# A kernel of attention and two feed-forward layers: the first pass's order is taken from a table of pieces, and ScalarE takes over squares, scaling and sums

## The chip, the cores and the metric

The kernel runs on one core of a Trainium2 chip. The metric is the device time of one execution in microseconds (us). The engines that matter are TensorE (PE in the profile; PEld is its loading of weights), VectorE (DVE), ScalarE (ACT), GpSimd (POOL) and SyncE (SP), which issues transfers. Each engine works through its own list of instructions in the order in which the program holds them; an instruction that waits holds up all that stand behind it on that engine.

## What is computed

```python
scores = scale * q_c @ k_c^T              # q, k, v: (4, 8, 576, 64), chunks of 64 positions
attn   = exp(scores - rowmax);  attn /= (rowsum + 1e-9)
x      = attn @ v_c                       # put together as 2304 tokens x 512
x      = (s * relu(x @ w_in)**2 + b) @ w_out       # layer 1, 512 -> 2048 -> 512
h      = x @ w2_in
out    = (h * tanh(softplus(h))) @ w2_out          # layer 2 (Mish)
```

All in float32; the matrix products of the layers are made of three products each, of a high and a low part (hi*hi, hi*lo, lo*hi).

## The kernel before

The 2304 tokens are 18 attention tiles of 128, and five blocks of 512, 256, 512, 512 and 512 tokens for the layers. The 2048 inner columns of a layer are 16 chunks of 128; four chunks form a group, and one pass takes one group through all five blocks. So there are eight passes (four for each layer) of 20 steps. A step is one chunk on one block: 12 matmuls into a hidden tile `hp` (`mm_in`, L331), the squaring or Mish, the splitting into `ghi` and `glo`, and 12 matmuls into the accumulators (`mm_out`, L368). At the end of a block the accumulators are added into `ysum` (L383 to L387).

In the first pass the attention runs beside layer 1. Each tile goes through: K and Q transposed on TensorE (`k_pe`, `q_pe`, L231) and copied out by ScalarE (L243 into the block diagonal `kbd`, L252 into `qt`); the scores (`s_pe`, L263); maximum and subtraction on VectorE (L274, L275); the exponential on ScalarE (L281); sum, reciprocal and normalising (L286 to L290, the last on GpSimd for three early tiles and on VectorE for the others); the result transposed (L231) and copied (L298); the product with V (`x_pe`, L308); and the hi and lo parts of x (L314 on ScalarE, L315 on VectorE). The weights are decoded from their loaded words as well: `abs` on ScalarE (L124), two clamps and shifts and two combinations on VectorE (L129 to L144), hi on ScalarE (L157), lo on VectorE (L162).

The order before comes from two hand-written strings and a loop. `LOADS` (L22) lists the first transfers, with V of tiles 0 to 3 issued from ScalarE's queue. `START` (L23) orders the first four tiles, with some dummy matmuls on zeros (`w3` is three of them) between the pieces. Then the loop at L468 takes one layer step after another; in step n it also does X of tile n+1, T (the transpose of the weights of the attention) of tile n+2, S of tile n+3, and K and Q of tile n+4. The rest of the first pass (three steps) and all the later passes are written at L528, and the framework's scheduler orders them. The PSUM banks of the loop's attention are two (`ps_t`), handed out in turn.

Of the kernel before, what the change touches and what calls it, by code (L numbers as in the profile page):

```python
# [15 lines left out]
P = 128  # L16
# [5 lines left out]
LOADS = "k0 q0 V0 k1 q1 V1 k2 q2 V2 W0 k3 q3 V3 W1 k4 q4 W2 W3 s0 k5 q5 v4 W4 W5 v5 W6 W7 v6"  # L22
START = (  # L23
    "w3 w5 K0 k0* Q0 q0 w3 K1 S0 k1* Q1 w1 m0 q1 e0 S1 n0 Q2 K2 K3 k2 m1 q2 e1 T0 S2 w3 n1 m2 Q3 k3 q3 T1 "
    "e2 t0 n2 t1 S3 X0 m3 T2 e3 X1 n3* A0 x0 w4 t2 T3 x1 t3 X2 A1 x2 B0 X3 w2 x3 w6 B1"
# [7 lines left out]
def chunk_attention_moe_moe_kernel(  # L33
# [44 lines left out]
    ps_t = ctx.enter_context(tc.tile_pool(name="ps_t", bufs=2, space=bass.MemoryType.PSUM))  # L78
# [7 lines left out]
    def x_tiles(b):  # L86
        xhi[b] = sb.tile([P, KD, sizes[b]], F32R, tag=f"xhi{b}", name=f"xhi{b}")
        xlo[b] = sb.tile([P, KD, sizes[b]], F32R, tag=f"xlo{b}", name=f"xlo{b}")

    def y_tile(b):  # L90
        ysum[b] = sb.tile([P, KD * sizes[b]], F32, tag=f"ysum{b}", name=f"ysum{b}")
# [18 lines left out]
    def decode_w(l, f, part):  # L110
        decode_a(l, f, part)
        decode_b(l, f, part)

    def decode_a(l, f, part):
        decode_a1(l, f, part)
        decode_a2(l, f, part)

    def decode_a1(l, f, part):
# [3 lines left out]
        u = a.bitcast(U32)  # L122
        if l == 1:
            nc.scalar.activation(out=a, in_=t[:, :, 1].bitcast(F32), func=AF.Abs)  # L124
        else:
            nc.vector.tensor_scalar(
                out=u, in0=t[:, :, 1], scalar1=0x7FFFFFFF, scalar2=None, op0=ALU.bitwise_and
            )
        nc.vector.tensor_scalar(  # L129
# [7 lines left out]
    def decode_a2(l, f, part):  # L137
# [36 lines left out]
    kbd = {}  # L174
# [53 lines left out]
    def transposes(i, src):  # L228
        p = ps_at(i, [P, KD, P])
# [16 lines left out]
    def q_pe(i):
        at[i]["qp"] = transposes(i, at[i]["q"].rearrange("p h d -> p (h d)"))

    def q_out(i, alt=False):
        at[i]["qt"] = sb_at(i, "qt").rearrange("p (a s) -> p a s", a=KD)  # L250
        eng = nc.vector.tensor_copy if alt else nc.scalar.copy
        eng(out=at[i]["qt"], in_=at[i].pop("qp"))  # L252
        if NS <= i and i + 2 < NTILE:
            load_qk(i + 2, "k")
            load_qk(i + 2, "q")

    def s_pe(i):
        t = at[i]
        t["sp"] = ps_at(i, [P, H, CH])
# [50 lines left out]
    def x_out(i, alt=False):  # L310
        xp = at.pop(i)["xp"]
        b, o = home[i]
        hi, lo = xhi[b][:, :, o:o + P], xlo[b][:, :, o:o + P]
        nc.scalar.activation(out=hi, in_=xp, func=AF.Copy)  # L314
        nc.vector.tensor_tensor(out=lo, in0=xp, in1=hi.bitcast(F32), op=ALU.subtract)  # L315
        if NS <= i and i + 3 < NTILE:
            load_v(i + 3)


    def mm_in(l, f, b, spare):  # L320

        n = sizes[b]
        pool, tag = (ps_t, "t") if spare and f % 2 else (ps_h, "h")
# [14 lines left out]
    def ew_a(l, hp, n):  # L338
        r = sb.tile([P, TB], F32, tag="tmp", bufs=2, name="r")[:, :n]
        if l == 1:  # L340
            nc.scalar.activation(out=r, in_=hp, func=AF.Relu)  # L341
            nc.vector.scalar_tensor_tensor(  # L342
                out=r, in0=r, scalar=s_sb[:, 0:1], in1=r, op0=ALU.mult, op1=ALU.mult
            )
# [4 lines left out]
    def ew_b(l, r, n):  # L349
        hi = sb.tile([P, TB], F32R, tag="ghi", bufs=3, name="ghi")[:, :n]  # L350
        lo = sb.tile([P, TB], F32R, tag="glo", bufs=3, name="glo")[:, :n]
        if l == 1:
            nc.scalar.activation(out=r, in_=r, func=AF.Identity, bias=b_sb[:, 0:1])  # L353
        nc.scalar.activation(out=hi, in_=r, func=AF.Copy)  # L354
        nc.vector.tensor_tensor(out=lo, in0=r, in1=hi.bitcast(F32), op=ALU.subtract)  # L355
        return hi, lo
# [17 lines left out]

    def add_up(l, grp, b, acc):

        t0, n = blocks[b]
        for m, a in enumerate(acc):
            w = n if l == 1 else DM
            y = ysum[b][:, m * w:(m + 1) * w]  # L380
            if grp == 0:
                if m % 2:
                    nc.vector.tensor_copy(out=y, in_=a[:, :w])  # L383
                else:
                    nc.scalar.copy(out=y, in_=a[:, :w])
# [18 lines left out]

    pend = []
    accs = {}

    def out_half(h):
        l, grp, b, f, g = pend[0]
        if h == 0 and f % FG == 0:  # L410
            accs[l, b] = [
                ps_acc.tile([P, TB], F32, tag=f"acc{m}", name=f"acc{m}")
                for m in range(KD if l == 1 else sizes[b] // P)
            ]
        mm_out(l, f, g, accs[l, b], sizes[b], h)
        if h == 1:
            pend.pop(0)
            if f % FG == FG - 1:
                add_up(l, grp % NG, b, accs.pop((l, b)))

    first, second = chunk_parts(0), chunk_parts(1)
    DECODE = {0: first[2:4], 1: first[4:6], 2: first[6:7], 3: first[7:8]}
    DECODE.update(zip((7, 9, 10, 11, 13, 14, 15, 16), ([z] for z in second)))
    with tc.manual_schedule():
        nc.scalar.preload_act_table_set("exp_and_others")
# [153 lines left out]
```

## Time and profile before

| | us |
|---|---|
| median of 3 runs | 922.19 (921.17 to 923.06) |
| the profiled execution | 922.06 |
| its span, first to last instruction | 920.3 |
| TensorE busy in the span | 880.0 (96%) |
| VectorE busy | 480.9 (52%) |
| ScalarE busy | 368.7 (40%) |
| last matmul ends at | 915.86 |

The span is read by stages: TensorE has idle time only before 203 us; from there to 915.86 us it is busy without a gap, and 4.4 us of last additions and stores follow. The 1.8 us between the span and the time of the execution lie around the program.

### The profile page before, as it was taken

The page shows a single profiled execution, that of the slowest core. Times are in us where ns is not written, and L with a number is a line of the kernel's source. Part 1 is how long each engine was busy: PE and PEld are TensorE (multiplying, and loading weights), DVE is VectorE, ACT ScalarE, POOL GpSimd, SP SyncE. Part 2 cuts the span into 40 slices and gives each one's busy share as a digit, 9 for nine tenths or more (in the row PEclk, how much of TensorE's full clock was granted, in tenths as well). Part 3 has the DMA queues.
Part 4 walks back from the last instruction along what each step waited for, and adds up shares of the span by engine and source line. Part 5 has one row for each costly group of instructions (what it writes and reads, how often), then busy time and mean ns, then how long its engine had stood idle before and what let it go on. Part 6 is the DMA issues. An engine that isn't in the chain of part 4 may idle for free.

```text
span 920.3 us, 12036 instructions
## 1 busy us (share of the span) xinstructions
PE 880.0 (96%) x4878; PEld 735.8 (80%) x4878; DVE 480.9 (52%) x851; ACT 368.7 (40%) x643; POOL 33.9 (4%) x33
## 2 busy tenths in 40 slices
PE   4878889999999999999999999999999999999998
PEld 4656777778888888888988888888888888888886
DVE  1767667768833694359635971166225932222223
ACT  1555556656543463334544542233222322222221
POOL 1100000000000000000212220000000000000000
PEclk7978999999999999999999999999999999999999
DMA  9524463205000410023001400041003200001012
GB/s 251 149 47 115 121 162 98 46 1 160 24 1 1 124 59 1 1 69 115 1 1 37 125 22 1 5 133 46 0 1 93 90 1 1 0 1 46 24 46 91
DMA packets 81526, 53.20 MB, mean 58 GB/s; under 512 B 58688, under 2 KB 75072, under 8 KB 81472
## 3 DMA queue, kind: packets, MB, share of 16 engines
q1 hardware_dynamic: 77120, 51.39, 19.1%
q10 hardware_dynamic: 4352, 1.05, 0.5%
q8 instruction: 38, 0.62, 0.3%
q14 instruction: 16, 0.13, 0.0%
HBM read 47.71 MB, written 4.72 MB: 57 GB/s over the span
## 4 chain that ended last, share of the span: by engine, by line
PE 82%; DVE 9%; ACT 5%; DMA 2%; issue 1%; POOL 0%; DVEq 0%; ACTq 0%; POOLq 0%
PE hp L331 41%; PE acc L368 39%; DMA v<-in_v_dram 2%; DVE wdec L144 1%; DVE wdec L140 1%; ACT e L281 1%; ACT kbd L243 1%; ACT w L157 1%; DVE sm L286 1%; DVE e L275 1%; DVE xlo L315 1%; DVE mx L274 1%; DVE e L290 1%; DVE w L162 1%; DVE wdec L132 1%
## 5 line engine op out<-in xcount | busy, mean ns | idle before, releaser
L331 PE MATMUL hp<-xhi,w 128*128 128x512 f32 (+1 forms) x1280 | 373.1, 373 | 2.6 <-ACT w L157 1.7
L331 PEld LDWEIGHTS hp<-xhi,w 128*128 128x128 f32 x1280 | 233.3, 190 | 47.1 <-issue 2.7
L331 PE MATMUL hp<-xlo,w 128*128 128x512 f32 (+1 forms) x640 | 237.6, 371 | 0.1
L355 DVE TENSOR_TENSOR glo<-r,ghi 128x512 fp32r<-128x512 f32 (+1 forms) x160 | 104.9, 656 | 215.3 <-ACT ghi L354 214.9
L368 PE MATMUL acc<-ghi,w 128*128 128x512 f32 (+1 forms) x640 | 164.8, 375 | 2.5 <-DVE w L162 1.9
L368 PE MATMUL acc<-w,ghi 128*128 128x512 f32 x576 | 159.6, 390 | 0.0
L346 ACT ACTIVATE r<-hp 128x512 f32<-128x512 f32 (+1 forms) x80 | 44.4, 555 | 255.1 <-PE hp L331 255.1
L331 PEld LDWEIGHTS hp<-xlo,w 128*128 128x128 f32 x640 | 121.6, 190 | 21.6 <-DVE xlo L315 0.8
L368 PEld LDWEIGHTS acc<-ghi,w 128*128 128x128 f32 x640 | 113.7, 190 | 22.1 <-DVE w L162 2.2
L368 PEld LDWEIGHTS acc<-w,ghi 128*128 128x128 f32 x576 | 106.9, 188 | 21.3
L387 DVE TENSOR_TENSOR ysum<-acc,ysum 128x512 f32<-128x512 f32 (+1 forms) x114 | 71.8, 655 | 59.5 <-PE acc L368 59.5
L341 ACT ACTIVATE r<-hp 128x512 f32<-128x512 f32 (+1 forms) x80 | 44.1, 551 | 132.1 <-PE hp L331 132.0
L354 ACT ACTIVATE ghi<-r 128x512 fp32r<-128x512 f32 (+1 forms) x160 | 94.1, 588 | 4.5
L368 PE MATMUL acc<-glo,w 128*128 128x512 f32 (+1 forms) x320 | 94.1, 370 | 0.0
L368 PE MATMUL acc<-w,glo 128*128 128x512 f32 x288 | 93.9, 389 | 0.0
L342 DVE SCALAR_TENSOR_TENSOR r<-r,s_sb 128x512 f32<-128x512 f32 (+1 forms) x80 | 56.4, 705 | 67.3 <-ACT r L341 67.2
L353 ACT ACTIVATE r<-r,b_sb 128x512 f32<-128x512 f32 (+1 forms) x80 | 54.6, 682 | 51.2 <-DVE r L342 51.0
L368 PEld LDWEIGHTS acc<-glo,w 128*128 128x128 f32 x320 | 58.4, 189 | 10.3
L368 PEld LDWEIGHTS acc<-w,glo 128*128 128x128 f32 x288 | 54.1, 188 | 11.3
L157 ACT ACTIVATE w<-wdec 128x512 fp32r<-128x512 f32 x64 | 40.3, 630 | 54.4 <-DVE wdec L144 54.0
L162 DVE TENSOR_TENSOR w<-wdec,w 128x512 fp32r<-128x512 f32 x64 | 44.9, 703 | 2.9 <-ACT w L157 2.0
L140 DVE SCALAR_TENSOR_TENSOR wdec<-wraw,wdec 128x512 uint32<-128x512 uint32 x64 | 44.0, 693 | 0.6
(302 smaller groups left out, 494.7 us busy)
## 6 DMA issues: line engine op xcount, KB each, us to landing
wraw<-in_moe_w_in_dram SPq DMA_DIRECT2D x32, 512.0 KB, 3.9
wraw<-in_moe_w_out_dram SPq DMA_DIRECT2D x32, 512.0 KB, 3.5
out_dram<-ysum SPq DMA_DIRECT2D x18, 256.0 KB, 2.0
k<-in_k_dram SPq DMA_DIRECT2D x16, 256.0 KB, 2.9
v<-in_v_dram SPq DMA_DIRECT2D x56, 64.0 KB, 3.3
q<-in_q_dram SPq DMA_DIRECT2D x12, 256.0 KB, 2.9
v<-in_v_dram ACTq DMA_DIRECT2D x16, 64.0 KB, 4.1
k<-in_q_dram SPq DMA_DIRECT2D x4, 256.0 KB, 4.8
```

The lines of the kernel that those rows point to most:

```text
L140: nc.vector.scalar_tensor_tensor(out=u, in0=t[:, :, 1], scalar=0xC0000000, in1=u, op0=ALU.bitwise_and, op1=ALU.bitwise_or,)
L157: nc.scalar.activation(out=w[:, 0], in_=a, func=AF.Copy)
L162: nc.vector.tensor_tensor(out=lo, in0=a, in1=hi.bitcast(F32), op=ALU.subtract)
L331: nc.tensor.matmul(out=hp, lhsT=w[:, sl], rhs=r[b][:, a, :], start=(a == 0 and p == 0), stop=(a == KD - 1 and p == 2),)
L341: nc.scalar.activation(out=r, in_=hp, func=AF.Relu)
L342: nc.vector.scalar_tensor_tensor(out=r, in0=r, scalar=s_sb[:, 0:1], in1=r, op0=ALU.mult, op1=ALU.mult)
L346: nc.scalar.activation(out=r, in_=hp, func=AF.Mish)
L353: nc.scalar.activation(out=r, in_=r, func=AF.Identity, bias=b_sb[:, 0:1])
L354: nc.scalar.activation(out=hi, in_=r, func=AF.Copy)
L355: nc.vector.tensor_tensor(out=lo, in0=r, in1=hi.bitcast(F32), op=ALU.subtract)
L368: nc.tensor.matmul(out=acc[m][:, :n] if l == 1 else acc[m], lhsT=w[wi][:, sl] if l == 1 else g[gi][:, sl], rhs=g[gi] if l == 1 else w[wi], ...
L387: nc.vector.tensor_tensor(out=y, in0=a[:, :w], in1=y, op=ALU.add)
```

## The change

The strings `LOADS` and the loop are gone. A new `START` names every piece of the whole first pass in one order, transfers included, and a function `pieces` issues them. A name is a kind and a number: `dk`, `dq`, `dv` are the loads of a tile; `K Q S T X` its parts on TensorE with `@` the PSUM bank; `k q m e n z t x y` the parts on ScalarE and VectorE (`z` is the normalising, now on VectorE for all tiles); `W a c d h l` load and decode a weight part; `I J` and `O P` are the halves of `mm_in` and `mm_out` of a step, `r u v g o` its elementwise parts, `E` the copy of an accumulator into `ysum`; `w13` is thirteen dummy matmuls. In all there are 76 dummy matmuls in the table, where there were 27.

Further: the squares of steps 0 to 7 are an `activation` with Square on ScalarE (`u`), and their scaling by s goes into the activation that adds b (`v`); the accumulators of blocks 0 and 1 are copied by ScalarE alone; three `kbd` buffers serve all tiles in turn, where tiles from 4 on had one; the attention uses up to six PSUM banks that the table names; V of tiles 1 to 3 is loaded from SyncE's queue; the first pass ends wholly before the second pass begins, and the last three of the 16 weight parts that the first pass decoded are decoded at the beginning of the second (`rest`).

```diff
-LOADS = "k0 q0 V0 k1 q1 V1 k2 q2 V2 W0 k3 q3 V3 W1 k4 q4 W2 W3 s0 k5 q5 v4 W4 W5 v5 W6 W7 v6"
 START = (
-    "w3 w5 K0 k0* Q0 q0 w3 K1 S0 k1* Q1 w1 m0 q1 e0 S1 n0 Q2 K2 K3 k2 m1 q2 e1 T0 S2 w3 n1 m2 Q3 k3 q3 T1 "
+    "dq0 dk0 dv0 W2 dk2 dq2 dq1 Q0@4 dk1 q0 w3 K0@5 dk3 k0.0 dq3 sb dv2 w13 S0@0 a2 c2 w2 K2@1 m0 k2.1 dq8 w3 "
...
+    "n7 J5 r3 O0 z9 r5 u3 z7 Q16@5 u5 m10 v3 P0 dq15 v5 q16 c7 I4 e10 K12@4 c4 g3 I7 k12.0 dk15 o3 J4 n10 J7 r4 "
...
-        eng = nc.gpsimd if i < NS and not alt else nc.vector
-        eng.tensor_tensor(out=e, in0=e, in1=sm.to_broadcast([P, H, CH]), op=ALU.mult)
...
+    def s_norm(i):
+        e = at[i]["e"]
+        nc.vector.tensor_tensor(out=e, in0=e, in1=at[i].pop("sm").to_broadcast([P, H, CH]), op=ALU.mult)
...
+    def ew_v(r, squared=False):
+        nc.scalar.activation(
+            out=r, in_=r, func=AF.Identity, scale=s_sb[:, 0:1] if squared else 1.0, bias=b_sb[:, 0:1]
+        )
...
+        elif name == "dv":
+            load_v(i, nc.sync if i else nc.scalar)
...
+        elif name == "u":
+            if i < 8:
+                nc.scalar.activation(out=ff[i]["r"], in_=ff[i]["r"], func=AF.Square)
+            else:
+                ew_u(ff[i]["r"])
...
+        elif name == "E":
+            first_sum(i, m, first_acc[i][m], nc.vector.tensor_copy if m % 2 and i >= 2 else nc.scalar.copy)
...
-    for grp in range(2 * NG):
+    for grp in range(1, 2 * NG):
...
+        rest = parts[13:] if grp == 1 else []
...
+            for z in rest[2 * step:2 * step + 2]:
+                decode_w(*z)
```

Where instructions stand now is shown at three places. First TensorE at the very start; `warm` is the output of the dummy matmuls, `ident` the identity of the transposes. Before:

```order
L445 MATMUL warm<-zero 128x128 x8
L231 MATMUL pa<-ident,k 128x128 x8
L445 MATMUL warm<-zero 128x128 x3
L231 MATMUL pa<-ident,k 128x128 x4
L263 MATMUL pa<-kbd,v 64x128 x8
```

and now:

```order
L246 MATMUL pt__103<-ident,q 128x128 x4
L468 MATMUL warm<-zero 128x128 x3
L246 MATMUL pt__113<-ident,q 128x128 x4
L468 MATMUL warm<-zero 128x128 x13
L272 MATMUL pa<-kbd,v 64x128 x8
L468 MATMUL warm<-zero 128x128 x2
```

The eight dummy matmuls that stood ahead of the first transposes are gone, and thirteen stand between the transposes of tile 0 and its scores.

Second, ScalarE at the start; L243 and now L257 are the copies that the first scores need. Before:

```order
L425 ACT_TABLE_LOAD
L224 DMA v<-in_v_dram 64x4x64 x16
L243 COPY kbd<-pa 64x8x64
L252 COPY v<-pa 128x512
L243 COPY kbd_161<-pa 64x8x64
```

and now:

```order
L498 ACT_TABLE_LOAD
L238 DMA v<-in_v_dram 64x4x64 x4
L264 COPY v<-pt__103 128x512
L257 COPY kbd<-pt__113 64x8x64 x2
L140 ACTIVATE wdec<-wraw 128x512
```

Twelve of the sixteen transfers that stood ahead of the first copy have left ScalarE's list (they are on SyncE's now).

Third, TensorE in the middle of the first pass: how a tile's small matmuls (L231, L263, L308) lie among those of the layer. Before, from block 1:

```order
L231 MATMUL pt__891<-ident,q 128x128 x4
L308 MATMUL pt__904<-e,v 64x64 x16
L331 MATMUL hp<-xhi_438,w 128x256 x2
L331 MATMUL hp<-xlo_439,w 128x256
...
L263 MATMUL pt__935<-kbd,qt 64x128 x8
L331 MATMUL hp<-xhi_438,w 128x256 x2
```

and now, ahead of the first use of the accumulators:

```order
L246 MATMUL pt__922<-ident,e 128x128 x4
L246 MATMUL pa<-ident,q 128x128 x4
L318 MATMUL pt__941<-e,v 64x64 x16
L246 MATMUL pa<-ident,k 128x128 x4
L272 MATMUL pt__979<-kbd_83,qt 64x128 x8
L318 MATMUL pa<-e,v 64x64 x16
L246 MATMUL pa<-ident,k 128x128 x4
L272 MATMUL pa<-kbd,qt 64x128 x8
L344 MATMUL hp<-xhi_321,w 128x512 x2
```

The small matmuls of several tiles now stand in a row, and there are fewer places at which TensorE goes over from them to the layer's.

## Rows read from the trace of the kernel before

**Rows 1.** Busy time by stretch: start:end, length, then each engine's busy us (instructions), clock, DMA.

```profile
0.00:202.89 202.89, 167.08 (x1513) 136.87 (x1513) 127.63 (x238) 105.74 (x192) 7.39 (x13) 0.92 0.44 112
106.00:202.89 96.89, 88.12 (x854) 71.46 (x852) 67.42 (x127) 58.21 (x108) 0.00 (x0) 1.00 0.35 88
202.89:915.86 712.97, 712.97 (x3366) 598.96 (x3366) 352.16 (x613) 262.97 (x452) 26.55 (x20) 1.00 0.13 41
135.06:144.44 9.38, 9.38 (x89) 7.51 (x85) 7.13 (x13) 5.08 (x10) 0.00 (x0) 1.00 0.35 95
207.40:212.84 5.44, 5.44 (x26) 4.50 (x25) 3.95 (x7) 3.07 (x6) 0.00 (x0) 1.00 0.56 151
242.75:244.19 1.44, 1.44 (x14) 1.43 (x12) 1.40 (x4) 0.74 (x2) 0.00 (x0) 1.00 0.00 0
157.17:166.87 9.70, 9.44 (x85) 7.49 (x85) 7.65 (x16) 5.72 (x10) 0.00 (x0) 1.00 0.40 90
217.78:244.09 26.31, 26.31 (x123) 21.98 (x123) 26.07 (x49) 18.88 (x33) 0.00 (x0) 1.00 0.28 89
```

**Rows 2.** Waits of TensorE, first 202 us: us in total, times, longest us.

```profile
PE pa L263 <- DVE kbd L243: 10.8, 1, 10.8
PE pt__519 L263 <- ACT qt L252: 3.7, 1, 3.7
```

**Rows 3.** Timeline of ScalarE's queue at the start: start us, us, instruction, count.

```profile
0.76 16.24 ACTq L224 DMA_DIRECT2D v<-in_v_dram  x16
```

**Rows 4.** Timeline of TensorE around step 16 of the first pass.

```profile
202.89 0.73 PE L331 MATMUL hp<-xhi,w 128*128 128x512 f32 x2 [0.94 <-ACT xhi L314]
```

**Rows 5.** Timeline of TensorE: small matmuls of a tile, each with the row behind it.

```profile
136.65 1.09 PE L263 MATMUL pt__1366<-kbd,qt 128*64 128x128 f32 x16
137.68 0.73 PE L331 MATMUL hp<-xhi,w 128*128 128x512 f32 x2
...
141.00 0.60 PE L231 MATMUL pt__1415<-ident,k 128*128 128x128 f32 x4
141.35 0.71 PE L368 MATMUL acc<-ghi,w 128*128 128x512 f32 x2
...
143.36 1.15 PE L308 MATMUL pt__1445<-e,v 64*64 64x64 f32 x32
144.44 0.73 PE L331 MATMUL hp<-xhi,w 128*128 128x512 f32 x2
```

**Rows 6.** Timeline of TensorE: dummy matmuls (two records each) and the first transposes.

```profile
1.05 3.79 PE L445 MATMUL warm<-zero 128*128 128x128 f32 x16 [1.05 <-DVE zero L439]
4.63 1.92 PE L231 MATMUL pa<-ident,k 128*128 128x128 f32 x8
...
38.37 2.05 PE L445 MATMUL warm<-zero 128*128 128x128 f32 x16
```

**Rows 7.** Timeline of VectorE within one step.

```profile
157.96 0.68 DVE L274 TENSOR_REDUCE mx<-pt__1590 128x8 f32<-128x512 f32 x1
...
159.29 0.74 DVE L342 SCALAR_TENSOR_TENSOR r<-r,s_sb 128x512 f32<-128x512 f32 x1
160.07 0.69 DVE L286 TENSOR_REDUCE sm<-e 128x8 f32<-128x512 f32 x1
...
161.23 0.69 DVE L290 TENSOR_TENSOR e<-e,sm 128x512 f32<-128x512 f32 x1
161.84 0.69 DVE L355 TENSOR_TENSOR glo<-r,ghi 128x512 fp32r<-128x512 f32 x1
```

**Rows 8.** ScalarE's activation of line 354, first 260 us: ns min/median/max.

```profile
L354 ACT ACTIVATE ghi<-r x28: 417/632/635, 49.3 to 257.1; 128x512 fp32r<-128x512 f32 x20, 128x256 fp32r<-128x256 f32 x8
```

**Rows 9.** Transfers of the first 35 us, and SyncE's issue of one tile's V.

```profile
DMA packets 22242, 8.96 MB, mean 256 GB/s; under 512 B 19689, under 2 KB 21737, under 8 KB 22241
...
k<-in_k_dram SPq DMA_DIRECT2D x5, 256.0 KB, 4.8
...
76.85 2.58 SPq L224 DMA_DIRECT2D v<-in_v_dram  x4
```

More of the change, by code (lines that the diff above doesn't have):

```diff
@@ L1 @@
+import re
 from contextlib import ExitStack
@@ L162, in decode_lo, with decode_w @@
         nc.vector.tensor_tensor(out=lo, in0=a, in1=hi.bitcast(F32), op=ALU.subtract)
+    def decode_w(*z):
+        for step in (decode_a, decode_c, decode_d, decode_h, decode_l):
+            step(*z)
     def runs(t0, n):
@@ L373, in mm_out, with first_sum @@
             )
+    def first_sum(b, m, a, eng):
+        y_tile(b)
+        n = sizes[b]
+        eng(out=ysum[b][:, m * n:(m + 1) * n], in_=a[:, :n])
     def add_up(l, grp, b, acc):
@@ L381, in add_up @@
             if grp == 0:
[L382 to L385, printed above, removed]
+                (nc.vector.tensor_copy if m % 2 else nc.scalar.copy)(out=y, in_=a[:, :w])
                 continue
@@ L421, in chunk_attention_moe_moe_kernel, with new_accs, pieces @@
-    first, second = chunk_parts(0), chunk_parts(1)
-    DECODE = {0: first[2:4], 1: first[4:6], 2: first[6:7], 3: first[7:8]}
-    DECODE.update(zip((7, 9, 10, 11, 13, 14, 15, 16), ([z] for z in second)))
+    parts = chunk_parts(0) + chunk_parts(1)
+    ff = {}
+    first_acc = {}
+    def new_accs(l, b):
+        return [
+            ps_acc.tile([P, TB], F32, tag=f"acc{m}", name=f"acc{m}")
+            for m in range(KD if l == 1 else sizes[b] // P)
+        ]
+    def pieces(name, i, m, bank):
+        b, f = divmod(i, FG)
+        n = sizes[b] if b < NB else 0
+        if name in ("dk", "dq"):
+            load_qk(i, name[1])
+        elif name == "dv":
+            load_v(i, nc.sync if i else nc.scalar)
+        elif name == "sb":
+            nc.sync.dma_start(out=s_sb, in_=s_in.partition_broadcast(P))
+            nc.sync.dma_start(out=b_sb, in_=b_in.partition_broadcast(P))
+        elif name in "KQSTX":
+            dict(K=k_pe, Q=q_pe, S=s_pe, T=p_pe, X=x_pe)[name](i, bank)
+        elif name == "k":
+            k_out(i, m)
+        elif name in "qmenztxy":
+            dict(q=q_out, m=s_max, e=s_exp, n=s_sum, z=s_norm, t=p_out, x=x_hi, y=x_lo)[name](i)
+        elif name in "Wacdhl":
+            dict(W=load_w, a=decode_a, c=decode_c, d=decode_d, h=decode_h, l=decode_l)[name](*parts[i])
+        elif name == "w":
+            for _ in range(i):
+                nc.tensor.matmul(out=warm[:, :P], lhsT=zero, rhs=zero)
+        elif name == "I":
+            ff[i] = {}
+            ff[i]["h"], ff[i]["half"] = mm_in(1, f, b, False)
+            ff[i]["half"](0)
+        elif name == "J":
+            ff[i]["half"](1)
+        elif name == "r":
+            ff[i]["r"] = ew_r(1, ff[i]["h"], n)
+        elif name == "u":
[3 more added lines that the diff above has]
+                ew_u(ff[i]["r"])
+        elif name == "v":
+            ew_v(ff[i]["r"], i < 8)
+        elif name == "g":
+            ff[i]["g"] = ew_g(ff[i]["r"], n)
+        elif name == "o":
+            ff[i]["o"] = ew_o(ff[i]["r"], ff[i]["g"], n)
+        elif name in "OP":
+            if name == "O" and f == 0:
+                first_acc[b] = new_accs(1, b)
+            mm_out(1, f, (ff[i]["g"], ff[i]["o"]), first_acc[b], n, "OP".index(name))
+        elif name == "E":
+            first_sum(i, m, first_acc[i][m], nc.vector.tensor_copy if m % 2 and i >= 2 else nc.scalar.copy)
+        else:
+            raise ValueError(name)
@@ L440, in chunk_attention_moe_moe_kernel @@
         make_identity(nc, ident)
-        warm = ps_t.tile([P, TB], F32, tag="t", name="warm")
-        def warm_up(n):
-            for _ in range(n):
-                nc.tensor.matmul(out=warm[:, :P], lhsT=zero, rhs=zero)
-        kbd[0] = atp.tile([P, KD, 2, P], F32, name="kbd")
+        warm = ps_h.tile([P, TB], F32, tag="h", name="warm")
         room = sb.tile([P, 2, KD, 2, P], F32, tag="ysum3", name="kbd12")
-        kbd[1], kbd[2] = room[:, 0], room[:, 1]
-        kbd[3] = sb.tile([P, KD, 2, P], F32, tag="ysum2", name="kbd3")
@@ L451, in chunk_attention_moe_moe_kernel @@
[L451 removed]
+        kbd = [atp.tile([P, KD, 2, P], F32, name="kbd"), room[:, 0], room[:, 1]]
+        for kb in kbd:
             nc.gpsimd.memset(kb, 0.0)
[L453 to L455 removed]
         for w in START.split():
[L457 removed]
```

260 lines of the change are left out of this document (83 added, 177 removed), and 20 rows, old and new, of the table START.

## The prediction, made before the changed kernel ran

> **What bounds the kernel now.** I read the busy time by stretch first. From 202.89 us to the last matmul at 915.86 us TensorE is busy for all 712.97 us [rows 1]. Before 202.89 us it is busy for 167.08 us, so 35.8 us of idle lie there, at a mean granted clock of 0.92. Only the first pass can be shortened, and everything it gains reaches the end, since nothing but TensorE's own work follows. At 202.89 us the layer matmuls of step 16 begin [rows 4]; by the loop's order the first pass then still has the first halves of steps 16 to 19 and the second halves of 15 (one part of two) to 19: 4 + 4.5 = 8.5 sets of twelve. A whole step takes 5.44 us, a set 2.72 us [rows 1], so 23.1 us are left and the first pass ends, in work, at 226.0 us. The other seven passes take 712.97 - 23.1 = 689.9 us, or 98.55 us each. Check: 16 steps of 5.44 us and 4 of 2.88 us (two sets of 1.44 us [rows 1]) are 98.6 us. Behind the last matmul lie 4.4 us, and 1.8 us around the span. So **time = end of the first pass + 696.1 us**, and before it is 226.0 + 696.1 = 922.1 us, 0.1 us from the median of the runs.
>
> What fills the 226.0 us? Next I read the waits and the timeline. Layer work is 98.6 us. A step with one tile beside it and no wait takes 9.38 us [rows 1], so a tile costs TensorE 9.38 - 5.44 = 3.94 us, and 18 of them 70.9 us. The 27 dummy matmuls take 0.256 us each at full speed (2.05 us for eight [rows 6]), 6.9 us. With 35.8 us of idle this is 212.2 us; the other 13.8 us are matmuls at 1.2 GHz instead of 2.4. The longest idle is 10.8 us in front of the first scores [rows 2]: ScalarE's first copy stood behind sixteen V transfers, whose issue held its queue for 16.24 us [rows 3].
>
> **The change, part by part.** The sum is of TensorE's own list in the first pass.
>
> *Layer matmuls*: unchanged, 98.6 us.
>
> *Attention*: the same matmuls, but what a tile costs is not all matmul. By start-to-start times, a group of four transposes takes 0.35 us, the scores 1.03, the product with V 1.08 [rows 5]: 3 x 0.35 + 1.03 + 1.08 = 3.16 us, 56.9 us for 18. The other 0.78 us of the 3.94 come where TensorE goes over from small matmuls to the layer's, four times in each tile (behind X, S, T and K), 0.2 us each. The table has 37 such places where the loop would have 72. I take 56.9 + 37 x 0.2 = 64.3 us; the ends are 56.9 and 70.9 us.
>
> *Dummy matmuls*: 76 x 0.256 = 19.5 us, 12.5 us more than before. They are on TensorE's list for good: where the wait that they fill is shorter than they are, they are a cost.
>
> *The start*: eight dummy matmuls no longer run ahead of the first transposes, which can start when the first load lands, about 4.6 us [rows 6]. At the start matmuls run at half speed whatever the clock column says: eight dummy matmuls took 3.79 us there, 0.47 us each, against 0.256 us later [rows 6]. That lasted from 1.05 to about 6.3 us. If it lasts as long from 4.6 us, 2.6 us are lost. Start: 7.2 us. The 10.8 us wait has no cause left: four transfers remain ahead of ScalarE's first copy, about 4 of the 16.24 us, over by 5 us. What is late next is the transposes of K of tile 0, then thirteen dummy matmuls that are longer than the two copies behind which they stand; they are in the sum.
>
> The Trainium skill (DMA: Bandwidth & Descriptors, "Issuing engines are not separate DMA queues") says that issuing on several engines saves only sequencer time, usually small. The trace agrees that issuing is the price, but it is not small here: 16.24 us of ScalarE [rows 3].
>
> *Transfers moved to SyncE*: twelve, of 2.58/4 = 0.65 us [rows 9], 7.7 us of a queue that all other loads share, spread over the first 20 us. The loads were also pulled forward. Up to Q of tile 16 the list holds 18.3 MB; at 256 GB/s [rows 9] plus 0.7 us of start and 4.8 us of landing that is 77 us. TensorE asks for it after 68.2 us of its list, 7.2 us of start and some 3 us of changes, at 78 us. It just holds. A K or Q load waits for the transposes two tiles before it (two buffers); between those TensorE has 6.1 us or more of listed work, over the 4.8 us of a landing. So transfers are costed at nothing, covered by 1 us; without that cover they cost what they are late.
>
> *VectorE*: after the first layer matmuls it is the engine next in line. One tile with one decoded weight part and one step's two operations kept it busy for 7.65 us [rows 1]: maximum and subtraction 1.33, squaring 0.67 to 0.74, sum to reciprocal 1.16, normalising 0.61, and 0.61 each for the lows of g and x [rows 7], which leaves 2.66 us for the decode. From I0 (the third of the layer's first halves) to P8 the table holds 7 maxima, 7 sums, 8 normalisings, 9 lows of x, 9 decodes, 9 lows of g (four of half size) and only 2 squarings: 57 us. TensorE's list there is 59.6 us and 26 of the 37 changes, 64.8 us. VectorE must be busy 0.88 of that time. It reached 26.07 of 26.31 us where work was always ready, and 7.65 of 9.70 us (0.79) in the loop [rows 1]. By the first there is no wait; by the second it needs 72.2 us and TensorE waits 7.4 us. The table keeps several tiles in flight, which is nearer to the first. I take a third of the way, **2.5 us**, ends 0 and 7.4.
>
> *Squares on ScalarE*: eight leave VectorE, four of 0.7 us and four smaller, and as many come to ScalarE at 0.63 us or less (taken from its pass over g [rows 8]); it was busy 5.72 of 9.70 us [rows 1], so they hide. Three normalisings come from GpSimd to VectorE (1.8 us) ahead of the first layer step, where it has room. The sums of blocks 0 and 1 are four copies that go to ScalarE, hidden likewise.
>
> The Trainium skill (ScalarE: Activation LUTs, "Rules for kernel authors") says to multiply on VectorE, not on ScalarE. By it the eight would go back: VectorE's 57 us would be 62, 0.96 of TensorE's time, and a third of the way 4.6 us. The same page ("What ACT_TABLE_LOAD costs") prices the second pointer operand of the scaling at 93 ns, an estimate of 0.7 us for eight, hidden too.
>
> *The second pass*: three decodes are left to it, 8 us of VectorE, while four sets of twelve (10.9 us) come first on TensorE. Taken as nothing; at worst 8 us.
>
> Sum: 98.6 + 64.3 + 19.5 + 7.2 = 189.6, with the wait 192.1 us. Time: 192.1 + 696.1 = **888 us**. Ends: 98.6 + 56.9 + 19.5 + 7.2 = 182.2, so 878.3 us; 98.6 + 70.9 + 19.5 + 7.2 + 7.4 = 203.6, so 899.7 us.
>
> **The rivals.** (1) *VectorE becomes the bound.* For it: 0.88 is asked, the loop gave 0.79, and 67.42 of 96.89 us (0.70) over its longer stretch [rows 1]. Against: there it waited on a loop that did one tile at a time. At 0.79 the wait is 7.4 us: 189.6 + 7.4 + 696.1 = 893 us; at 0.70 it is 16.6 us: 902 us. (2) *Loads come late.* One queue, 1 us of cover. If the three tightest loads (Q of 12, K of 16, Q of 16) each come one landing late, 3 x 4.8 = 14.4 us: 900 us. (3) *Slower: the clock.* With many small matmuls of several tiles in a row, each waiting a little on other engines, the granted clock falls to 1.2 GHz between I0 and P8 and stays; the 64.8 us become 129.6: 189.6 + 64.8 + 696.1 = 950 us. It decides from 36.4 us of full-speed work done at half speed. For it: waits such as 3.7 us [rows 2] were followed by half speed, the 13.8 us above. Against: from 106 to 202.89 us TensorE idled for 8.8 us in small waits and the clock stayed at 1.00 [rows 1]. (4) *It doesn't do what it says*: the first pass is shorter, but what it left undone is paid at the start of the second, 8 us: 894 us; to come out the same it would have to be 34 us.
>
> **How the numbers follow.** Forecast, 880 to 893 us: 0.52. Rival 1, 893 to 904: 0.24. Rival 2, 893 to 902: 0.11. Rival 4: 0.04 at 893 to 898 and 0.01 as no change. Rival 3: 0.03. Better than 880 us: 0.05. Left out by 878 to 902 us: 0.03 below, 0.07 of rivals 1 and 2 above, 0.04 of the no change and the slower one; I keep this range. 0.2% is 1.8 us, about what runs of this kernel can tell from no change. Faster 0.96, same 0.01, slower 0.03.
>
> **What would show it.** The first scores at about 12 us instead of 18.55; the first layer matmul at 38 to 41 us; TensorE idle for less than 15 us in the first pass; the last accumulator of the first pass copied near 192 us and no gap in TensorE's work afterwards; the clock at 1.00 from about 10 us on. Waits of TensorE on VectorE's lows between 60 and 125 us speak for rival 1, on K or Q copies behind a transfer for rival 2, a clock of 0.5 for rival 3. I am wrong altogether if the second pass has gaps, or if a piece waits for one that stands far behind it in another engine's list.

## The result, and the profile after

The changed kernel takes 892.1 us (median of 4 runs, 891.0 to 895.2) against 921.7 us for the kernel before on the same chip: a ratio of 0.968, 95% interval 0.966 to 0.971. That is 29.6 us less; 888 us was forecast, and the range was 878 to 902 us.

The profiled execution took 891.04 us, its span is 889.3 us. First its busy time by stretch, with the columns of [rows 1]: the first pass, the rest, the stretch in which the prediction looked for VectorE (from I0 to the end of P8), and the busiest time of the DMA engines.

```profile
0.00:195.31 195.31, 187.29 (x1712) 160.09 (x1713) 123.86 (x229) 120.48 (x217) 3.38 (x9) 0.99 0.53 134
195.31:884.90 689.59, 689.50 (x3265) 579.80 (x3263) 347.20 (x610) 254.72 (x441) 26.58 (x20) 1.00 0.12 38
67.11:131.82 64.71, 64.15 (x650) 54.56 (x648) 55.54 (x106) 51.13 (x99) 0.00 (x0) 1.00 0.48 108
40.00:80.00 40.00, 39.44 (x442) 33.69 (x441) 30.58 (x57) 31.81 (x59) 0.00 (x0) 0.97 0.96 268
```

The first pass now ends at 195.3 us (before: 226.0 in work). TensorE idles 8.0 us in it instead of 35.8, at a mean clock of 0.99 instead of 0.92. Behind it TensorE is busy without a gap, as before: 689.6 us. So all of the gain lies in the first pass, 30.7 us of it, and nothing is paid later.

These are all of TensorE's waits in its first 230 us (us in total, times, longest), in place of the 10.8 and 3.7 us of [rows 2]:

```profile
PE pt__103 L246 <- DMA q<-in_q_dram: 3.9, 1, 3.9
PE pa L246 <- DMA k<-in_k_dram: 2.9, 1, 2.9
PE pt__400 L246 <- DMA q<-in_q_dram: 0.6, 1, 0.6
PE pt__941 L318 <- ACT e L308: 0.3, 1, 0.3
PE pa L246 <- DMA q<-in_q_dram: 0.3, 1, 0.3
```

7.7 of the 8.0 us are waits for loads of Q and K. No wait for VectorE is left. The start of ScalarE and of TensorE, in place of [rows 3, 6] (start us, us, instruction):

```profile
0.76 2.74 ACTq L238 DMA_DIRECT2D v<-in_v_dram  x4
...
3.91 1.08 PE L246 MATMUL pt__103<-ident,q 128*128 128x128 f32 x4 [3.91 <-DMA q<-in_q_dram]
4.79 1.48 PE L468 MATMUL warm<-zero 128*128 128x128 f32 x6
6.07 1.06 PE L246 MATMUL pt__113<-ident,q 128*128 128x128 f32 x4
6.92 3.61 PE L468 MATMUL warm<-zero 128*128 128x128 f32 x26
10.46 1.09 PE L272 MATMUL pa<-kbd,v 128*64 128x128 f32 x16
```

V holds ScalarE's queue for 2.74 us instead of 16.24, and the first scores start at 10.46 us instead of 18.55. Last, the one large wait inside the pass, and the row behind it:

```profile
37.67 0.63 PE L246 MATMUL pa<-ident,k 128*128 128x128 f32 x4 [2.91 <-DMA k<-in_k_dram]
...
38.57 4.02 PE L468 MATMUL warm<-zero 128*128 128x128 f32 x20
42.52 1.09 PE L272 MATMUL pa<-kbd,qt 128*64 128x128 f32 x16
43.55 0.73 PE L344 MATMUL hp<-xhi,w 128*128 128x512 f32 x2
```

K of tile 8 is late. Behind the wait ten dummy matmuls take 3.95 us (38.57 to 42.52) instead of the 2.56 us that ten cost at the prediction's price: TensorE is at its lower clock for most of them (mean granted clock 0.57 in that stretch).

### The profile page after: what moved, and what is told of

Read it like the earlier page. It is cut to its first block, busy times and chain, and to the rows that moved or that the text cites. A ratio compares the mean times of both kernels' runs of the same rounds, so it can differ in the third digit from the quotient of the medians.

```text
span 889.3 us, 12265 instructions
## 1 busy us (share of the span) xinstructions
PE 876.8 (99%) x4976; PEld 739.9 (83%) x4976; DVE 472.1 (53%) x840; ACT 375.2 (42%) x657; POOL 30.0 (3%) x29
## 4 chain that ended last, share of the span: by engine, by line
PE 97%; DMA 2%; SPq 0%; DVE 0%; issue 0%; ACT 0%; DVEq 0%
PE hp L344 44%; PE acc L397 44%; PE warm L468 2%; DMA q<-in_q_dram 1%; PE pa L246 1%; PE pa L272 1%; DMA k<-in_k_dram 1%; PE pa L318 0%; SPq L238 0%; DVE ysum L418 0%; SPq L225 0%; PE pt__103 L246 0%; PE pt__1546 L318 0%; PE pt__1212 L318 0%; PE pt__1966 L318 0%
## 5 line engine op out<-in xcount | busy, mean ns | idle before, releaser
L344 PE MATMUL hp<-xhi,w 128*128 128x512 f32 (+1 forms) x1280 | 368.9, 369 | 0.0
L397 PE MATMUL acc<-ghi,w 128*128 128x512 f32 (+1 forms) x640 | 162.1, 371 | 0.0
L360 DVE SCALAR_TENSOR_TENSOR r<-r,s_sb 128x512 f32<-128x512 f32 (+1 forms) x72 | 51.6, 717 | 60.6 <-ACT r L354 60.5
L365 ACT ACTIVATE r<-r,b_sb 128x512 f32<-128x512 f32 (+1 forms) x72 | 49.5, 688 | 48.6 <-DVE r L360 48.3
L397 PEld LDWEIGHTS acc<-w,glo 128*128 128x128 f32 x288 | 54.1, 188 | 11.3
```

Source lines behind the costliest of these rows:

```text
L344: nc.tensor.matmul(out=hp, lhsT=w[:, sl], rhs=r[b][:, a, :], start=(a == 0 and p == 0), stop=(a == KD - 1 and p == 2),)
L360: nc.vector.scalar_tensor_tensor(out=r, in0=r, scalar=s_sb[:, 0:1], in1=r, op0=ALU.mult, op1=ALU.mult)
L365: nc.scalar.activation(out=r, in_=r, func=AF.Identity, scale=s_sb[:, 0:1] if squared else 1.0, bias=b_sb[:, 0:1])
L397: nc.tensor.matmul(out=acc[m][:, :n] if l == 1 else acc[m], lhsT=w[wi][:, sl] if l == 1 else g[gi][:, sl], rhs=g[gi] if l == 1 else w[wi], ...
```

## The experiments

Two theories were to be told apart. **Engines**: VectorE is next in line, as the prediction had it, and the dummy matmuls cost what they are longer than their waits. **Loads**: SyncE's transfers pace the first pass until K and Q are in, and work that is taken from the other engines comes back as a wait for a load. All kernels ran beside the kernel before; ratios are to that, with 95% intervals. The changed kernel's is 0.968 (0.966 to 0.971).

**1. Squares and sums back on VectorE**

```
-            if i < 8:
-                nc.scalar.activation(out=ff[i]["r"], in_=ff[i]["r"], func=AF.Square)
-            else:
-                ew_u(ff[i]["r"])
+            ew_u(ff[i]["r"])
...
-            ew_v(ff[i]["r"], i < 8)
+            ew_v(ff[i]["r"])
...
-            first_sum(i, m, first_acc[i][m], nc.vector.tensor_copy if m % 2 and i >= 2 else nc.scalar.copy)
+            first_sum(i, m, first_acc[i][m], nc.vector.tensor_copy if m % 2 else nc.scalar.copy)
```

> The changed kernel, with the squares of the first eight steps multiplied and scaled on VectorE again and the odd sums of blocks 0 and 1 copied by VectorE, as in the kernel before. Theory A (VectorE has slack, as no wait of TensorE on VectorE is in the trace of the changed kernel): within 0.7 us of the changed kernel. Theory B (VectorE is next in line, as the prediction had it): 2 to 5 us more, with waits of TensorE on VectorE's operations between 60 and 130 us.

Measured: 893.7 us, 0.969 (0.967 to 0.971). That is 1.6 us more than the changed kernel, between the two theories; the intervals overlap, so the two kernels can't be told apart. No wait for VectorE; beside the start (4.0 us, here put down to GpSimd at the same place) TensorE waits for loads only, K of tiles 8 and 14 and Q of tile 7:

```profile
PE pa L246 <- DMA k<-in_k_dram: 5.2, 2, 2.8
PE pt__103 L246 <- POOL kbd L503: 4.0, 1, 4.0
PE pa L246 <- DMA q<-in_q_dram: 1.3, 1, 1.3
```

Loads hide the answer here, so it was asked again in experiment 6.

**2. The 49 dummy matmuls behind 20 us taken out**

```
-... e3 w11 K11@4 ... dq6 w7 K5@2 ... n5 w10 S8@3 ... W10 w17 X5@2 ... l3 w4 X11@4 ...
+... e3 K11@4 ... dq6 K5@2 ... n5 S8@3 ... W10 X5@2 ... l3 X11@4 ...
```

> The changed kernel without the five groups of dummy matmuls behind 20 us (11, 7, 10, 17 and 4 of them, 49 in all, 14.0 us of TensorE as measured there). Theory A (they are on the list for good and cost what they are longer than the wait that they fill): K of tiles 11 and 5, the copy of K of tile 8 and the copy of tile 5's transposed weights would have made TensorE wait about 2.3, 1.4, 1.0 and 1.6 us anyway, so 6 to 8 us less. Theory B (they hold the clock up through the waits): the waits come back, TensorE falls to the lower clock behind them, and the kernel takes 2 to 10 us more. Theory C (all of them stand where a load or a copy is awaited): within 1.5 us.

Measured: 892.4 us, 0.969 (0.967 to 0.971): by start-to-start times in the changed kernel 13.0 us of TensorE's list are gone (not 14.0, as expected), and the time stays. In TensorE's timeline waits stand in their place, among them two at 69 and 76 us, far behind the last dummy matmul:

```profile
69.01 0.63 PE L246 MATMUL pa<-ident,q 128*128 128x128 f32 x4 [2.11 <-DMA q<-in_q_dram]
...
76.32 1.09 PE L246 MATMUL pa<-ident,k 128*128 128x128 f32 x4 [2.91 <-DMA k<-in_k_dram]
77.34 1.98 PE L272 MATMUL pa<-kbd,qt 128*64 128x128 f32 x16
```

The second is K of tile 14, followed by the scores of tile 7 at the lower clock (1.98 instead of 1.09 us). TensorE came there sooner and waited for the load. The expected outcome nearest to this is that of theory C, but its reason is only half true: the waits that the dummy matmuls had covered returned, and what was saved beyond them was lost at 69 and 76 us. Not all of the returned waits are for loads: of 15.7 us behind the start 9.7 end with a load and 6.0 with a copy or a normalising on ScalarE or VectorE (the longest, 3.0 us, behind a weight decode that had itself waited 1.8 us for its load).

**3. V of tiles 11 and 5 behind K of tile 8**

```
-... m3 dv11 a1 ... X2@1 dv5 k5.2 ... x1 h1 K6@0 ... l1 q6 dq4 ...
+... m3 a1 ... X2@1 k5.2 ... x1 h1 dv5 K6@0 ... l1 q6 dv11 dq4 ...
```

> The changed kernel, with the V transfers of tiles 11 and 5 issued behind Q of tile 6 and behind K and Q of tile 8 instead of ahead of K of tile 8; V5 and V11 are first used only after 50 us. Theory A (the order of SyncE's list holds up K of tile 8): its load is issued about 3 us earlier (at 29 instead of 32.2 us), lands at about 34 us, TensorE's wait of 2.9 us in front of it shrinks to under 0.5 us, the ten dummy matmuls behind it run at full speed (2.6 instead of 4.0 us): 3 to 4.5 us less. Theory B (the transfers are limited by bandwidth, not by the queue that issues them): the load lands as late as before, within 1 us of the changed kernel's time.

Measured: 894.7 us, 0.971 (0.970 to 0.973); not faster, and perhaps slower. The wait for K of tile 8 is indeed gone, and the first layer matmul starts at 39.59 instead of 43.55 us. But loads further back are late instead:

```profile
PE pa L246 <- DMA k<-in_k_dram: 4.4, 4, 2.4
PE pt__103 L246 <- DMA q<-in_q_dram: 3.9, 1, 3.9
PE pa L246 <- DMA q<-in_q_dram: 2.5, 2, 1.6
PE pt__569 L246 <- DMA k<-in_k_dram: 0.6, 1, 0.6
```

Theory A was right on the single wait and wrong on the time.

**4. V of tiles 1 to 3 back on ScalarE's queue**

```
-            load_v(i, nc.sync if i else nc.scalar)
+            load_v(i, nc.sync if i >= NS else nc.scalar)
```

> The changed kernel, with the V transfers of tiles 1 to 3 issued by ScalarE again (twelve, at the same places of the table) instead of SyncE. Theory A (the issue holds ScalarE's copies and exponentials back): each tile's four transfers hold its queue for 2.6 to 3.4 us between 8 and 22 us, where TensorE's small matmuls wait for ScalarE; 3 to 9 us more. Theory B (SyncE's queue is the tighter one): SyncE is 8.6 us less busy, the waits for Q and K of 4.1 us inside the first pass go, and the kernel takes 1 to 4 us less.

Measured: 899.2 us, 0.976 (0.974 to 0.978), 7 us more. ScalarE's queue and TensorE's scores of tile 1, which wait for ScalarE's copies of K and Q behind the V transfers (start us, us):

```profile
16.52 5.55 ACTq L238 DMA_DIRECT2D v<-in_v_dram  x3
...
22.65 0.57 ACT L264 COPY qt<-pa 128x512 f32<-128x512 f32 x1
...
24.91 1.98 PE L272 MATMUL pa<-kbd,qt 128*64 128x128 f32 x16 [6.28 <-issue]
...
81.73 0.63 PE L246 MATMUL pa<-ident,k 128*128 128x128 f32 x4 [2.81 <-DMA k<-in_k_dram]
```

The scores of tile 1 start 7.0 us later than in the changed kernel (17.93 us). By the scores of tile 8 half of this is made up (45.9 against 42.5 us), but SyncE was held up too: from 24.0 to 34.3 us it issues nothing, as its next load waits for a buffer that TensorE has not read yet. K of tile 14 is issued at 78.3 instead of 71.0 us, and TensorE waits 2.81 us for it (last row). The Trainium skill (DMA: Bandwidth & Descriptors, "Issuing engines are not separate DMA queues") says that another issuing engine saves only sequencer time. The trace agrees that it is the issuing that counts, but that time costs 7 us here.

**5. Seven weight parts of the second pass later, then also without the dummy matmuls**

```
-... W4 W11 a0 ... dq10 W10 W15 a5 ... W8 dv6 ... dk14 W13 a7 W12 dq12 W14 dq16 ... dk12 dv12 ...
+... W4 a0 ... dq10 a5 ... dv6 ... dk14 a7 dq12 dq16 ... dk12 W12 dv12 ... dk13 W10 ... dq14 W8 ...
+... dq15 W11 ... dv10 W13 ... dk17 W14 W15 ...
```

> The changed kernel, with seven weight parts of the second pass (512 KB each, 3.7 MB) issued behind K of tile 12 and later instead of between 43 and 75 us; the dummy matmuls stay. Theory A (up to about 80 us the first pass runs at the pace of the loads, 0.96 of the DMA engines' time in 40 to 80 us, and the dummy matmuls fill that wait): the load waits near 70 and 78 us go, but the dummy matmuls still stand in TensorE's list, so only 0 to 3 us less than the changed kernel. Theory B (the loads are not the bound): within 0.5 us.

Measured: 887.3 us, 0.964 (0.962 to 0.965), 4.8 us less than the changed kernel, and more than theory A allowed.

> The seven weight parts late as in the run before, and the 49 dummy matmuls behind 20 us taken out as in the second experiment. Theory A (loads set the pace, so that taking the dummy matmuls out alone only turned them into waits): now the time goes too: the load waits of 2.1 and 2.9 us near 69 and 76 us are gone, 4 to 8 us less than the changed kernel. Theory B (loads are not the bound; what replaced the dummy matmuls is the chain of copies and reductions of single tiles on ScalarE and VectorE): within 1.5 us of the changed kernel.

Measured: 886.0 us, 0.962 (0.961 to 0.964), 6.1 us less than the changed kernel, as theory A had it, though only 1.3 us of this come with the dummy matmuls (887.3 against 886.0 us, and the runs of the two overlap). This is the lowest median of all. From 40 to 80 us the DMA engines are now busy 0.88 of the time at 216 GB/s, not 0.96 at 268. TensorE goes through the place of the second experiment's waits without a stop:

```profile
66.02 0.60 PE L246 MATMUL pa<-ident,q 128*128 128x128 f32 x4
...
70.68 0.66 PE L246 MATMUL pa<-ident,k 128*128 128x128 f32 x4
71.27 1.09 PE L272 MATMUL pa<-kbd,qt 128*64 128x128 f32 x16
```

The first row is Q of tile 7, the last the scores of tile 7, the twelfth in the table's order, right behind K of tile 14. The start of these scores decides the time to within some 2 us, as a table of starts read from TensorE's timelines shows (us):

| kernel | sixth scores (tile 8) | twelfth scores (tile 7) | span | span less twelfth |
|---|---|---|---|---|
| changed kernel | 42.5 | 76.1 | 889.3 | 813.2 |
| squares on VectorE (1) | 39.9 | 77.9 | 891.8 | 813.9 |
| no dummy matmuls (2) | 38.2 | 77.3 | 892.2 | 814.9 |
| V of 11 and 5 late (3) | 38.6 | 78.5 | 892.7 | 814.2 |
| V on ScalarE (4) | 45.9 | 82.3 | 896.1 | 813.8 |
| weights late (5) | 40.1 | 73.6 | 886.3 | 812.7 |
| weights late, no dummies (5) | 38.4 | 71.3 | 884.0 | 812.7 |

With the weights early, the kernels of experiments 1 to 3 reach the sixth scores 2.6 to 4.3 us sooner than the changed kernel and the twelfth 1.2 to 2.4 us later. With 3.7 MB moved behind, 2.5 to 4.8 us come through. Behind the twelfth scores all take 812.7 to 814.9 us. The clean pair is that without dummy matmuls: sixth scores at 38.2 and 38.4 us, twelfth at 77.3 us with the weights early and at 71.3 us with them late, 892.4 against 886.0 us.

In the pair with dummy matmuls the gain is not made where the weights were: from the sixth to the twelfth scores both kernels take 33.6 us. Its 2.5 us lie ahead, where with late weights K of tile 8 happens to be there 0.8 us sooner and the ten dummy matmuls behind it take 2.33 us (granted clock 1.00) instead of 3.95:

```profile
37.74 2.40 PE L468 MATMUL warm<-zero 128*128 128x128 f32 x20
40.07 1.09 PE L272 MATMUL pa<-kbd,qt 128*64 128x128 f32 x16
```

What the late weights do is that such a gain is kept, where experiments 1 to 3 lost it. Why the clock held here, one trace doesn't show.

Bytes are not all of the pace of the loads. In the second experiment SyncE itself waits 3.4 us at 55 us to issue a weight part, until ScalarE has read the buffer that it goes into, and in the third and the first 2.6 and 2.3 us; with the weights late there is no such wait before 70 us (SyncE then waits 3.3 and 3.5 us for a buffer that TensorE's scores free, further ahead of what TensorE needs). How much of the 6 us are bytes, how much issuing and how much such waits was not separated.

```profile
SPq L132 <- ACT wdec L140: 3.4, 1, 3.4
```

**6. Squares and sums on VectorE where the loads leave room**

Edit: that of experiment 1, on the fastest kernel of experiment 5.

> The run with seven late weight parts and without the 49 dummy matmuls (886.0 us), and with the squares of the first eight steps and the odd sums of blocks 0 and 1 on VectorE again. Theory A (VectorE has slack in the first pass even where the loads no longer hold it back): within 0.7 us of 886.0. Theory B (VectorE is next in line once the loads are out of the way): 1.5 to 5 us more, with waits of TensorE on VectorE between 60 and 130 us.

Measured: 886.7 us, 0.963 (0.961 to 0.964), against 886.0. VectorE's row for the stretch from I0 to the end of P8, which lies earlier here, is now

```profile
62.93:127.49 64.56, 64.01 (x649) 54.59 (x648) 60.81 (x119) 47.04 (x88) 0.00 (x0) 1.00 0.56 138
```

VectorE is busy 60.81 of 64.56 us, 0.94, and TensorE idles 0.55 us, 0.3 us of it behind VectorE. So moving the squares to ScalarE is worth less here than can be measured.

**7. A better order of the loads in the first 45 us**

First, the edit of experiment 3 was made on the fastest kernel of experiment 5:

> As the run before, and V of tiles 11 and 5 behind K of tile 8 as in the first experiment. Theory A (the loads' order counts once the bytes in front are fewer): the waits for K of tiles 11, 5 and 8 (2.6 and 1.3 us without the dummy matmuls) shrink, a further 1 to 3 us less. Theory B: within 0.7 us of the run before, as other loads become late in their place.

Measured: 890.2 us, 0.966 (0.965 to 0.968): 4.2 us more than without it. Theory B there, and worse: V of tile 11 now stands ahead of a weight part that ScalarE decodes, and TensorE waits 4.0 us for the copy behind that.

Then two kernels, both without the 49 dummy matmuls and with late weights, that go by the use of each load. The first puts V of tile 1 behind Q of tile 5, and K of tile 8 and Q of tile 11 ahead of V of tiles 5 and 11; the second also K and Q of tile 4 ahead of V of tiles 8 and 11.

```
 first:  ... dk5 ... dq5 dv1 ... dk6 ... dq6 ... k5.2 dk8 dq11 dv5 ... W3 X3@5 dv8 dv11 ... dk4 ... dq4 ...
 second: ... dk5 ... dq5 dv1 ... dk6 ... dq6 ... k5.2 dk8 dq11 dv5 ... W3 ... K6@0 dk4 ... dq4 dv8 ... dk9 dv11 ...
```

> The run with seven late weight parts and without the 49 dummy matmuls (886.0 us), and with five loads of the first 35 us in another order: V of tile 1 behind K and Q of tile 5, K and Q of tile 8 and 11 ahead of V of tiles 5 and 11. No load gets further behind than its use needs: V of tile 5 is issued some 15 us ahead of its first matmul. Theory A (the waits for K of tiles 11, 5 and 8, 1.4, 2.2 and 1.4 us, are made by the order of SyncE's list): 2 to 5 us less than 886.0. Theory B (as in the run with late V, whatever comes early there makes another load late): within 1 us, or slower.

Measured: 888.2 us, 0.965 (0.963 to 0.966).

> As the run with five loads reordered (888.2 us), and K of tile 4 and Q of tile 4 ahead of V of tiles 8 and 11 as well, with K issued as soon as K of tile 6 is transposed. There the only large wait left was 6.4 us for K of tile 4, whose load stood behind eight V transfers. Theory A (SyncE's order in the first 45 us made the waits; each load now stands where its use asks for it): that wait is under 1 us, 4 to 6 us less than 888.2, so 882 to 884, faster than any kernel so far. Theory B (to 45 us so many bytes and transfers are asked for that one load or another is late in any order): 886 us or more, with another load's wait in its place.

Measured: 888.1 us, 0.963 (0.962 to 0.965): not faster than the simple delay of the weights. In the first kernel TensorE's waits in front of 35 us shrink, and one of 6.37 us for K of tile 4 appears. In the second that one is down to 2.65 us, and a weight part comes late, for which ScalarE waits ahead of a copy that TensorE needs (timeline of the second kernel):

```profile
47.25 0.66 ACT L140 ACTIVATE wdec<-wraw 128x512 f32<-128x512 f32 x1 [4.54 <-DMA wraw<-in_moe_w_in_dram]
...
49.63 1.97 PE L318 MATMUL pa<-e,v 64*64 64x64 f32 x32 [4.88 <-ACT e L308]
```

The last row names ScalarE, but ScalarE's copy stood behind a decode that waited for a load. Theory B held: up to 50 us some load is late in each order tried.

**8. Parts of the change in the kernel before**

```
-LOADS = "k0 q0 V0 k1 q1 V1 k2 q2 V2 W0 k3 q3 V3 W1 ...
+LOADS = "k0 q0 V0 k1 q1 v1 k2 q2 v2 W0 k3 q3 v3 W1 ...
```

> The kernel before, with the V transfers of tiles 1 to 3 issued by SyncE at the same places of the list of loads, instead of ScalarE; nothing else. Theory A (the 16.24 us in which ScalarE issues V are the cause of the late first scores, and the later loop gives nothing back): first scores at about 12 instead of 18.55 us, 5 to 8 us less than the kernel before. Theory B (SyncE's queue takes over the delay, its later loads come 8 us later): within 2 us of the kernel before.

Measured: 912.6 us, 0.991 (0.990 to 0.993): 8.4 us less than the kernel before, a little more than theory A allowed. The first scores start at 7.24 instead of 18.55 us, 11.3 us sooner; by the fourth (24.1 against 30.4 us) 5 of them are lost again, above all in a wait for a load that is now issued behind V:

```profile
PE pa L231 <- DMA k<-in_k_dram: 3.6, 1, 3.6
```

The other part is the squares of its first eight steps and the odd sums of two blocks on ScalarE (the edit for the squares; the scaling and the sums follow the change's own):

```
...
             nc.scalar.activation(out=r, in_=hp, func=AF.Relu)
+            if sq:
+                nc.scalar.activation(out=r, in_=r, func=AF.Square)
+                return r
...
```

> The kernel before, with the squares and the scaling of its first eight steps on ScalarE and the odd sums of blocks 0 and 1 copied by ScalarE: this part of the change alone. Theory A (the prediction's: these hide, VectorE is not the bound): within 1.5 us of the kernel before. Theory B (VectorE, busy 0.70 to 0.79 in the loop, is relieved): 2 to 5 us less. Theory C (in the loop's order each further pass of ScalarE stands in one tile's chain): 1 to 4 us more.

Measured: 924.5 us, 1.004 (1.002 to 1.005): 3.5 us more. About 3 of them arise at one place, at which TensorE waits for ScalarE. In the kernel before:

```profile
133.99 1.15 PE L308 MATMUL pt__1331<-e,v 64*64 64x64 f32 x32 [1.68 <-ACT kbd L243]
```

and in this one:

```profile
134.41 1.97 PE L308 MATMUL pt__1331<-e,v 64*64 64x64 f32 x32 [1.68 <-ACT kbd L243]
...
139.16 1.87 PE L263 MATMUL pt__1366<-kbd,qt 128*64 128x128 f32 x16
```

The wait is 1.68 us in both, but here the lower clock follows, up to the scores at 139.16 us (1.87 instead of 1.09 us): the mean granted clock is 0.51 from 134 to 141 us, and 1.00 in the kernel before from 133 to 140 us. In the loop's order the squares on ScalarE bring nothing. Whether the extra time is theirs, or that of a clock which happened to fall in the profiled execution, one trace doesn't settle; the interval says that the kernel is slower.

## Why the prediction was right, and where it was not

*The accounting held.* "First pass + 696.1 us" gives 195.3 + 696.1 = 891.4 us; the execution took 891.0. No gap follows the first pass, so rival 4 is out; rival 3, the clock, is out too: 0.99 in the first pass.

*The sum came out 3.2 us short*, 192.1 against 195.3. By terms, from the timeline of the changed kernel: 11 groups of dummy matmuls fill 20.4 us (19.5 forecast). The start costs 3.9 us of waiting and some 0.9 us of slow transposes, 4.8 (7.2 forecast): the load of Q landed sooner than the 4.6 us taken for it, and part of the slow time falls on dummy matmuls. Waits inside the pass are 4.1 us (2.5 forecast). With 98.6 us for the layer, attention and changes are what remains: 195.3 - 98.6 - 20.4 - 4.8 - 4.1 = 67.4 us (64.3 forecast, ends 56.9 and 70.9). That term was mis-sized by 3.1 us. So the close number is in part luck: the start and the wait for VectorE were put 4.9 us too high, the other waits, the dummy matmuls and the attention 8.1 us too low. The reason for the attention is in these rows:

```profile
24.84 0.60 PE L246 MATMUL pt__337<-ident,k 128*128 128x128 f32 x4
25.28 0.60 PE L246 MATMUL pa<-ident,e 128*128 128x128 f32 x4
25.72 1.73 PE L468 MATMUL warm<-zero 128*128 128x128 f32 x14
...
63.74 0.60 PE L246 MATMUL pa<-ident,k 128*128 128x128 f32 x4
64.10 0.71 PE L344 MATMUL hp<-xhi,w 128*128 128x512 f32 x2
64.65 0.40 PE L344 MATMUL hp<-xlo,w 128*128 128x512 f32 x1
64.88 0.62 PE L344 MATMUL hp<-xhi,w 128*128 128x512 f32 x2
65.34 0.40 PE L344 MATMUL hp<-xlo,w 128*128 128x512 f32 x1
65.67 1.09 PE L272 MATMUL pa<-kbd,qt 128*64 128x128 f32 x16
```

Four transposes take 0.36 us only where layer matmuls follow; with another small group behind them they take 0.44 us and up to 0.6. I read 0.35 off a place of the first kind [rows 5], and charged only the changes to layer matmuls. Added up by start-to-start times, the 54 groups of transposes take 24.2 us (without the slow time of the start) where 0.35 each makes 18.9: 5.3 us more. The layer's matmuls take 104.2 us, 5.6 more than 98.6, where the 37 changes were put at 7.4: a pair of them behind a small group takes 0.55 instead of 0.46 us, and the last one ahead of the scores 0.33 instead of 0.23. Scores and products with V are 0.3 us below their price.

*The engine that was feared was the wrong one.* VectorE's work was sized well: 57 us in 64.8 us of TensorE's time were forecast from I0 to P8, 55.54 in 64.71 us were measured, a share of 0.86 against 0.88. The step that failed is the next one, from a busy share to a wait ("a third of the way, 2.5 us"): at 0.86 TensorE never waited for it, and at 0.94 (experiment 6) for 0.3 us. A likely reason, which no run isolates, is that the table puts several other pieces between a VectorE operation and its use. The share reached in the old loop said nothing on that.

*The waits were rival 2's.* It was put at 0.11 and 900 us. Its mechanism is what bounds the first pass up to 76 us, at a much smaller size: 3.8 us of waits for loads inside the pass, because 13.0 us of dummy matmuls cover the rest, and with it waits for copies (experiment 2). The text found the narrow place: loads up to Q of tile 16 by 77 us, TensorE asking at 78. The experiments show it at K of tile 14, 76 us. The wrong step was "transfers are costed at nothing, covered by 1 us": the cover was read as an excess of the table over the loads, but the loads are the pace. By the table only 8 of the 37 changes stand ahead of Q of tile 16, 1.6 us and not "some 3", so TensorE would have asked at 68.2 + 7.2 + 1.6 = 77.0 us: by the prediction's own terms there was no cover. What is taken off TensorE ahead of 76 us is not gained while the weights are early, as experiments 2 and 3 measured.

*The signs that were named.* No gap followed, TensorE's idle time stayed under 15 us, and the waits were for loads, as the sign of rival 2 had it. Two signs did not come: the first layer matmul began at 43.55 us and not at 38 to 41, behind the wait for K of tile 8, and the clock fell once after 10 us, at the same place.

*Where the 30.7 us come from*, on the prediction's terms: idle 35.8 to 8.0, 27.8 us less; dummy matmuls 6.9 to 20.4, 13.5 more; attention and changes 70.9 to 67.4, 3.5 less; the half-speed time of 13.8 us nearly gone, what is left of it lying in the terms above. 27.8 - 13.5 + 3.5 + (13.8 - 0.9) = 30.7. Of the 29.6 us between the medians V on SyncE alone is 8.4 us in the old order; squares and sums give nothing in either order. So about 21 us are left for the table itself, its pulled-forward loads, its dummy matmuls and its three `kbd` buffers. No run takes one of these alone back to the kernel before, so that this part is read off the accounting above and not shown by an experiment.

## What to carry to other kernels

Before an engine's work is counted as a gain, take out something large on it and look: if the time stays and waits for loads appear further on, the loads are the pace, and then it helps to have fewer transfers ahead of the point of need (here 3.7 MB of weights that were not due yet: 4.8 us with the dummy matmuls and 6.4 us without). Reordering such loads among themselves moved the wait from one to the next in each order tried. A high busy share is no wait: ask how many other pieces lie between an operation and its use.

## What the runs showed of the hardware that was not expected

- Small transfers hold the DMA engines longer for their bytes. From 0 to 30 us, where mostly K, Q and V move, the engines are busy 0.79 of the time for 189 GB/s (first row); from 45 to 60 us, mostly weights, 1.07 for 325 GB/s: 239 and 304 GB/s for a full share. The Trainium skill (DMA: Bandwidth & Descriptors, "Specifications") names 512 bytes as the least transfer for the full rate. The trace agrees as far as two stretches go: of the packets 18738 of 19380 are under that in the first, 4275 of 6648 in the second.

```profile
0.00:30.00 30.00, 25.45 (x274) 23.58 (x275) 16.01 (x34) 17.21 (x29) 3.38 (x9) 1.00 0.79 189
45.00:60.00 15.00, 15.00 (x189) 13.23 (x187) 12.13 (x24) 12.96 (x24) 0.00 (x0) 1.00 1.07 325
```

The packets of the two stretches:

```profile
DMA packets 19380, 5.67 MB, mean 189 GB/s; under 512 B 18738, under 2 KB 19250, under 8 KB 19378
DMA packets 6648, 4.88 MB, mean 325 GB/s; under 512 B 4275, under 2 KB 6203, under 8 KB 6644
```

- The clock after a wait is not set by the wait's length alone: a wait of 1.68 us at the same place was followed by full speed in one kernel and by half speed in another (experiment 8). And the clock column shows 1.00 from 0 to 30 us, while dummy matmuls took 0.43 us each at 4.8 us and 0.22 us each at 25.7 us (seven in 1.56 us).
